# Reading the first expert matrix in memory order for the early lists, and the second in runs of 1 KB to match

## The chip, the core and the metric

The kernel runs on one core of one Trainium2 chip. Its time is the device time of one execution in microseconds (us), as the median of several runs. A profile of one further execution shows the engines: TensorE (PE; PEld are its weight loads), VectorE (DVE), ScalarE (ACT), GpSimd (POOL), and SyncE (SP), which issues most of the DMAs. Each engine works through its own instructions in a fixed order, and waits where a semaphore of another engine or of a DMA has not come yet.

## The reference

Eight sequences of 2496 rows with 256 features go through a spectral layer, and the 19968 rows that come out go through a mixture of eight experts, in which each expert takes at most 2496 rows:

```python
X = np.fft.rfft(x, axis=1)
Yr = X.real @ w_r - X.imag @ w_i + b_r          # and Yi alike
Y = shrink(Yr) + 1j * shrink(Yi)                # by lam = 0.01
x = np.fft.irfft(Y, n=2496, axis=1).reshape(19968, 256)
logits = x @ w_gate                             # 8 columns
# pairs (token, expert) in order of falling logit: a token goes to the
# first expert that still has room (cap = 2496)
for e in range(8):
    h = np.maximum(x[assigned == e] @ w1[e], 0)  # w1[e] is 256 x 1024
    out[assigned == e] = h @ w2[e]               # w2[e] is 1024 x 256
```

The 1024 hidden features of an expert can stand in any order, if the columns of w1 and the rows of w2 have the same one.

## The kernel before

Three kinds of work follow each other and overlap. The spectral layer (`phase_a`) takes the eight sequences as batches, each through small Fourier matrices on PE, with intermediate results that ACT and DVE copy and subtract, POOL in part, and that are written to and read from memory. While the last batches are in it, `Router.early` finds for each expert 512 tokens of the first four batches that surely belong to it: these are the eight early lists, numbered 0 to 7 here. `Router.closing` then settles the experts one after the other, with long searches on DVE that use a tiny count on PE in each step; the tokens of an expert that were not in its early list form its late list, up to 1984 of them.

`Experts.run` works through a list in tiles of 128 tokens and chunks of 512. POOL gathers the rows of the spectral result (L581), PE transposes them (L596), and then comes for each of the eight blocks of 128 hidden features the first product (L611, 512 columns wide, fp32 made of a high and a low part, so six matmuls), an ACT copy with the positive part (L614) and a DVE step for the low part (L615). The second product takes the eight blocks as stationary operands (L627, 24 matmuls of 256 columns for a tile), ACT copies the result out (L630) and POOL scatters it (L634).

`Experts.load` brings in the two matrices of an expert. Each comes in two halves of 512 KB (m = 0, 1) through a ring of two raw tiles of 128 x 1024 (their slots are called xt in the profile, as the spectral part used them before). For an early list SP issues the loads (L557); for a late list the expert is known only on the chip, so POOL gathers rows of 4 KB (L559). Each half is then split: ACT copies it into the high part (L567), which rounds it, and DVE subtracts that from the raw half to get the low part (L568). The first matrix lives in slots called sh, the second in slots called FG. A raw tile is free for the next load when DVE's split of it is done.

How the halves lie matters for the change. A partition of the first matrix's raw half holds one row of w1, 1024 hidden features in memory order. `part` (L562) reads it as `p (k t) -> p t k` with t = 8: for block t the features t, t + 8, t + 16, and so on, 8 elements apart, and writes them side by side. So block t holds the features 8k + t. The second matrix is loaded to fit: partition p takes the rows 8p to 8p + 7 of w2, four in each half, which are one run of 4 KB in memory, and its split reads and writes in order.

The order of the instructions on every engine is set when the program is built. Each step is added to a planner (`Plan`) with an engine, a cost, a position and the buffers that it reads and writes; the planner simulates the engines and emits the steps in the order that comes out. A split costs the planner 0.95 us on ACT and 0.068 + 1024 / 960 us on DVE, for either matrix. ACT's and DVE's queues hold the splits of one list, the L614 and L615 steps of another and the steps of the router one behind the other; PE's holds the counts of the router (L412, L413) among the matmuls.

Of the kernel before, what the change touches and what calls it, by code (L numbers as in the profile page):

```python
# [266 lines left out]
class Kit:  # L267
# [17 lines left out]
    def v(self, n, pos, emit, reads, writes): return self.plan.add('V', 0.068 + n / 960, pos, emit, reads, writes)  # L285
# [252 lines left out]
class Experts:  # L538
# [8 lines left out]
    def load(self, pos, e=None, wi=None):  # L547

        K, plan, v = self.K, self.K.plan, self.K.v
        W1, W2 = K.sb("W1", [128, 2, 2, 1024], F32R), K.sb("W2", [128, 2, 8, 256], F32R)  # L550
        for k in range(2):
            for m in range(2):
                r = K.sb("raw", [128, 1024])
                p = pos + (2 * k + m)
                if e is not None:
                    src = self.w[k][e].rearrange("(p m) f -> p m f", m=2)[:, m] if not k else self.w[k][e].rearrange("(p g m) d -> p g (m d)", g=2, m=4)[:, m]
                    K.dma(p, lambda r=r, src=src: K.nc.sync.dma_start(r.t, src), 524e3, [], [r])  # L557
                else:
                    K.ind(p, lambda r=r, k=k, m=m: K.P.indirect_dma_start(out=r.t, out_offset=None, in_=self.rows[k],  # L559
                                                                          in_offset=bass.IndirectOffsetOnAxis(ap=wi.t[:, m:m + 1], axis=0)), 524e3, [wi], [r])  # L560

                def part(i, k=k, m=m, r=r):  # L562
                    if k: return W2.t[:, i - 1, 4 * m:4 * m + 4] if i else r.t.rearrange("p (m d) -> p m d", m=4)
                    return W1.t[:, i - 1, m].rearrange("p (t k) -> p t k", t=8) if i else r.t.rearrange("p (k t) -> p t k", t=8)
                W = (W1, W2)[k]
                h = plan.buf(None, None)
                plan.add('A', .95, p + 1, lambda part=part: K.A.copy(part(1), part(0)), [r], [W, h])  # L567
                v(1024, p + 1, lambda part=part: K.V.tensor_tensor(part(2), part(0), part(1), op=OP.subtract), [r, h], [W])  # L568
        return W1, W2
# [796 lines left out]
```

## Time and profile before

| | |
|---|---|
| median of 3 runs | 1635.14 us (1633.94 to 1639.24) |
| the profiled execution | 1637.3 us, of which 1635.5 us lie between its first and its last instruction (the span) |
| mean granted TensorE clock | 0.984 |
| instructions | 31215 |
| on the chain that ended last | PE 31%, issue 12%, DVE 6%, POOL 4%, ACT 2%, DMA 2%, by share of the span |
| DMA | 210.64 MB in 134489 packets, mean 129 GB/s |
| the first and the last early split of the first matrix on ACT | 505.1 us and 779.4 us |

Times in the profile count from the span's start. A row of an engine's timeline gives the start and the length in us, the engine, the line of the kernel, the operation, the tile that it writes and those that it reads, the shapes, how many instructions are merged in the row, and in brackets the idle time before it with what ended it. Names of tiles are slots, which different parts of the program share in turn. A PE that is busy is not always a PE at full rate, since its records overlap.

### The profile page before, as it was taken

The page shows a single profiled execution, that of the slowest core. Times are in us where ns is not written, and L with a number is a line of the kernel's source. Part 1 is how long each engine was busy: PE and PEld are TensorE (multiplying, and loading weights), DVE is VectorE, ACT ScalarE, POOL GpSimd, SP SyncE. Part 2 cuts the span into 40 slices and gives each one's busy share as a digit, 9 for nine tenths or more (in the row PEclk, how much of TensorE's full clock was granted, in tenths as well). Part 3 has the DMA queues.
Part 4 walks back from the last instruction along what each step waited for, and adds up shares of the span by engine and source line. Part 5 has one row for each costly group of instructions (what it writes and reads, how often), then busy time and mean ns, then how long its engine had stood idle before and what let it go on. Part 6 is the DMA issues. An engine that isn't in the chain of part 4 may idle for free.

```text
span 1635.5 us, 31215 instructions
## 1 busy us (share of the span) xinstructions
PE 1543.4 (94%) x10980; PEld 1381.9 (84%) x10980; DVE 1181.4 (72%) x3652; ACT 882.4 (54%) x1875; POOL 607.8 (37%) x726
## 2 busy tenths in 40 slices
PE   6999999999999967989899999999999999999997
PEld 3899999998798845878788888888889899889997
DVE  2777777778988885688988989988777766552331
ACT  1568788787688764454634434444344443563331
POOL 1114343343344556212342623534325253473112
PEclk8999999999999988999999999999999999999999
DMA  8877787887686564323221302211122211231000
GB/s 239 237 248 249 224 248 221 251 248 204 216 235 223 165 186 139 113 90 105 90 79 44 101 25 72 71 67 61 44 75 70 72 61 62 84 115 46 20 25 27
DMA packets 134489, 210.64 MB, mean 129 GB/s; under 512 B 31183, under 2 KB 94367, under 8 KB 134129
## 3 DMA queue, kind: packets, MB, share of 16 engines
q1 hardware_dynamic: 112468, 145.53, 29.7%
q0 software_dynamic: 21856, 63.04, 12.3%
q8 instruction: 88, 1.44, 0.4%
q14 instruction: 77, 0.63, 0.1%
HBM read 123.75 MB, written 84.75 MB: 127 GB/s over the span
## 4 chain that ended last, share of the span: by engine, by line
PE 31%; issue 12%; DVE 6%; POOL 4%; ACT 2%; DMA 2%; POOLq 0%; ACTq 0%
PE ps L627 14%; PE ps L611 10%; PE p L611 5%; POOL out_dram L634 3%; DMA xt<-in_moe_w_dram,wi 2%; DVE sh L568 2%; ACT sh L567 1%; PE ps L596 1%; DVE junk L402 1%; DVE FG L568 1%; ACT FG L567 0%; PE p L499 0%; POOL xt L559 0%; DVE yTl L615 0%; ACT ajunk L504 0%
## 5 line engine op out<-in xcount | busy, mean ns | idle before, releaser
L1010 PE MATMUL ps<-wt,xTh 128*128 128x256 f32 x1280 | 242.9, 289 | 0.0
L1010 PEld LDWEIGHTS ps<-wt,xTh 128*128 128x128 f32 x1280 | 200.8, 192 | 2.9 <-issue 0.2
L1010 PE MATMUL ps<-wt,xTl 128*128 128x256 f32 x640 | 181.3, 283 | 0.0
L868 POOL TENSOR_TENSOR s2l<-s2c,s2h 120x512 fp32r<-120x512 f32 (+1 forms) x96 | 118.0, 1233 | 142.7 <-ACT s2h L865 136.5
L634 POOL DMA_INDIRECT out_dram<-xTh,li x64 | 71.2, 1113 | 263.1 <-ACT xTh L630 235.5
L1087 POOL TENSOR_TENSOR yTl<-yr,yTh 128x468 bf16<-128x468 f32 (+1 forms) x88 | 98.8, 1122 | 165.8 <-ACT yTh L1084 114.9
L402 DVE SCALAR_TENSOR_TENSOR junk<-h_m,st,h_AG 128x156 bf16<-128x156 f32 (+1 forms) x472 | 157.9, 380 | 2.5
L1010 PEld LDWEIGHTS ps<-wt,xTl 128*128 128x128 f32 x640 | 122.2, 191 | 0.0
L630 ACT COPY xTh<-ps 128x256 f32<-128x256 f32 x80 | 29.9, 373 | 149.1 <-PE ps L627 127.3
L627 PE MATMUL ps<-FG,yTh 128*128 128x256 f32 (+1 forms) x504 | 108.8, 283 | 0.0
L991 PE MATMUL ps<-FG,sh 128*128 128x128 f32 x640 | 97.0, 282 | 8.4 <-DMA sh<-T 8.0
L991 PEld LDWEIGHTS ps<-FG,sh 128*128 128x128 f32 x640 | 88.4, 195 | 16.5 <-issue 9.5
L630 ACT COPY xTl<-ps 128x256 f32<-128x256 f32 x80 | 29.8, 372 | 126.7 <-PE ps L627 120.6
L634 POOL DMA_INDIRECT out_dram<-xTl,li x64 | 64.9, 1014 | 86.8 <-ACT xTl L630 77.8
L627 PE MATMUL ps<-FG,yTl 128*128 128x256 f32 (+1 forms) x368 | 88.3, 283 | 0.0
L568 DVE TENSOR_TENSOR sh<-xt,sh 128x1024 fp32r<-128x1024 f32 x32 | 69.4, 2182 | 17.9 <-ACT sh L567 17.8
L627 PEld LDWEIGHTS ps<-FG,yTh 128*128 128x128 f32 (+1 forms) x504 | 80.7, 187 | 0.7
L627 PE MATMUL ps<-FG,s2c 128*128 128x256 f32 (+1 forms) x356 | 80.4, 284 | 0.0
L1016 DVE TENSOR_TENSOR ps<-ps,bt 128x512 f32<-128x512 f32 x80 | 55.5, 694 | 30.7 <-PE ps L1010 25.6
L868 DVE TENSOR_TENSOR xl<-xt,xh 117x512 fp32r<-117x512 f32 (+1 forms) x77 | 61.0, 794 | 22.3 <-ACT xh L865 20.2
L1057 PE MATMUL p<-s2h,d 120*117 120x512 f32 (+1 forms) x192 | 76.7, 408 | 0.3 <-DVE s2h L865 0.3
L611 PE MATMUL ps<-y,sh 128*128 128x512 f32 (+1 forms) x187 | 71.5, 400 | 3.6 <-DVE yTl L615 1.6
(648 smaller groups left out, 5162.8 us busy)
## 6 DMA issues: line engine op xcount, KB each, us to landing
sh<-T SPq DMA_DIRECT2D x40, 512.0 KB
T<-s4st SPq DMA_DIRECT2D x80, 256.0 KB
s2c<-T SPq DMA_DIRECT2D x80, 240.0 KB
YD<-yst SPq DMA_DIRECT2D x80, 234.0 KB
T<-s1st SPq DMA_DIRECT2D x73, 240.0 KB
xt<-in_moe_w_dram SPq DMA_DIRECT2D x32, 512.0 KB
xt<-in_x_dram SPq DMA_DIRECT2D x105, 156.0 KB
LG<-lgst SPq DMA_DIRECT2D x80, 21.9 KB
```

What stands on the lines that cost most here:

```text
L402: v(cols + 59, p, lambda k=k: V.scalar_tensor_tensor(junk[k % 2].t[:, 0:cols], H.m[:, 0:cols], c.t[:, k // ng:k // ng + 1], ag(k % ng)[:, ...
L568: v(1024, p + 1, lambda part=part: K.V.tensor_tensor(part(2), part(0), part(1), op=OP.subtract), [r, h], [W])
L611: T.matmul(ps.t[:, 0:w], lhsT=W1.t[:, a, m, 128 * ft:128 * ft + 128], rhs=x_.t[:, 0:w], start=q + m == 0, stop=q + m == 3)
L627: T.matmul(ps.t[0:M], lhsT=a.t[:, 128 * q:128 * q + M], rhs=W2.t[:, w_, ft], start=k == 0, stop=k == 23)
L630: plan.add('A', .27, pos + 1, lambda: A.copy(o.t[0:M], ps.t[0:M]), [ps], [o])
L634: ins = P.indirect_dma_start(out=self.out, out_offset=bass.IndirectOffsetOnAxis(ap=oi.t[0:M, oo + t:oo + t + 1], axis=0), in_=o.t[0:M], in ...
L868: lambda: eng.tensor_tensor(lb[1](), src(), hb[1](), op=OP.subtract), [srcb, hb[0]], [lb[0]])
L991: T.matmul(ps.t[:, i, 128 * dt:128 * dt + 128], lhsT=sh.t[:, k, 128 * dt:128 * dt + 128], rhs=Ft.t[:, k], start=True, stop=True)
L1010: T.matmul(ps3.t[:, i], lhsT=a.t[:, i, dt, o:o + 128], rhs=wt[c].t[:, w, dt], start=n == 0, stop=n == 11)
L1016: plan.add('V', dve(512), pos + 1.282, lambda ps3=ps3: V.tensor_tensor(ps3.t, ps3.t, bt[:, None, :].to_broadcast([128, 2, 256]), op=OP.add ...
L1057: T.matmul(ps.t[0:M, gs_], lhsT=d5[0:k_, a, 0:M], rhs=v.t[0:k_, gs_], start=i == 0, stop=i == 2)
L1087: yq.append(plan.add('P', pool(2 * W), pos + 0.376, lambda yh=yh, yl=yl, yr=yr, W=W: P.tensor_tensor(yl.t[:, :, 0:W], yr.t[:, :, 0:W], yh. ...
```

## The change

Only the loads of the early lists change, in two places that belong together. The split of a first matrix's half reads the raw tile in memory order, so that block t holds the features 128 t to 128 t + 127. The second matrix is loaded to match: partition p takes for block t the row 128 t + p of w2, so a half is made of four runs of 1 KB per partition, 512 runs in place of 128 runs of 4 KB. Both kinds of split write to the same places as before, and the matmuls read the same tiles. The late lists, whose loads are gathered, keep the order that they had.

```diff
                 if e is not None:
-                    src = self.w[k][e].rearrange("(p m) f -> p m f", m=2)[:, m] if not k else self.w[k][e].rearrange("(p g m) d -> p g (m d)", g=2, m=4)[:, m]
-                    K.dma(p, lambda r=r, src=src: K.nc.sync.dma_start(r.t, src), 524e3, [], [r])
+                    src = self.w[k][e].rearrange("(p m) f -> p m f", m=2)[:, m] if not k else self.w[k][e].rearrange("(g m p) d -> p g m d", g=2, m=4)[:, m]
+                    K.dma(p, lambda r=r, src=src, k=k: K.nc.sync.dma_start(r.t.rearrange("p (m d) -> p m d", m=4) if k else r.t, src), 524e3, [], [r])
...
                 def part(i, k=k, m=m, r=r):
                     if k: return W2.t[:, i - 1, 4 * m:4 * m + 4] if i else r.t.rearrange("p (m d) -> p m d", m=4)
-                    return W1.t[:, i - 1, m].rearrange("p (t k) -> p t k", t=8) if i else r.t.rearrange("p (k t) -> p t k", t=8)
+                    return W1.t[:, i - 1, m].rearrange("p (t k) -> p t k", t=8) if i else r.t.rearrange("p (k t) -> p t k" if e is None else "p (t k) -> p t k", t=8)
```

The costs that the planner is given do not change, and the instructions of all engines stand in the same order as before. In SP's queue the sixteen loads of second matrices have another shape (128 x 4 x 256 in place of 128 x 1024); nothing else differs.

## The prediction

> **What bounds the kernel now.** I began with the page. TensorE (PE) is the busiest engine of the whole, at 94%, so what matters is where it is not busy.
>
> ```profile
> PE 1543.4 (94%) x10980; PEld 1381.9 (84%) x10980; DVE 1181.4 (72%) x3652; ACT 882.4 (54%) x1875; POOL 607.8 (37%) x726
> ```
>
> Next the windows: start and end, length, busy time with count of PE, PEld, DVE, ACT and POOL, granted clock, DMA share, GB/s. Six of the eight early lists fall into 640 to 800, the change to the late lists into 800 to 840, the late lists into the rest.
>
> ```profile
> 640.00:800.00 160.00, 147.21 (x961) 129.52 (x960) 126.08 (x415) 79.60 (x115) 37.44 (x55) 0.98 0.31 101
> 800.00:840.00 40.00, 34.50 (x226) 30.00 (x226) 37.57 (x163) 23.20 (x56) 26.63 (x31) 1.00 0.40 122
> 840.00:1635.00 795.00, 772.62 (x5214) 698.57 (x5212) 525.61 (x2068) 328.21 (x751) 292.06 (x403) 1.00 0.18 59
> ```
>
> PE idles 12.8 us in the first stretch, 5.5 us in the second, and 22.4 us in the 795 us behind. From 840 on PE sets the pace, so time won ahead of that should reach the end, if DVE and POOL have the late lists' data ready as much earlier.
>
> The rows of the two split lines come third (minimum, median and maximum ns, first and last start). sh are the slots of the first matrix, FG those of the second.
>
> ```profile
> L567 ACT CAST sh<-xt x32: 2075/2246/2431, 505.1 to 1426.7; 128x1024 fp32r<-128x1024 f32 x32
> L567 ACT CAST FG<-xt x32: 1037/1048/1112, 570.1 to 1447.1; 128x1024 fp32r<-128x1024 f32 x32
> ...
> L568 DVE TENSOR_TENSOR sh<-xt,sh x32: 2003/2186/2354, 507.3 to 1429.0; 128x1024 fp32r<-128x1024 f32 x32
> L568 DVE TENSOR_TENSOR FG<-xt,FG x32: 1205/1225/1950, 574.6 to 1448.2; 128x1024 fp32r<-128x1024 f32 x32
> ```
>
> Shape, types and engines agree; only the order in which the raw tile is read differs. Read 8 elements apart, a split takes 2246 ns on ACT and 2186 on DVE; read in order, 1048 and 1225.
>
> Last, PE's timeline, rows with idle time before them (in brackets, with what ended it): lists 0 and 1 in the spectral part, lists 2 to 7 behind, and one of the first late list.
>
> ```profile
> 510.62 0.39 PE L1027 MATMUL ps<-zl,fg 128*128 128x256 f32 x1 [0.85 <-DVE zl L1020]
> 516.95 0.62 PE L1077 MATMUL pt<-h_idn,yst 117*128 117x117 f32 x4 [0.56 <-DVE yr L1082]
> ...
> 594.10 0.55 PE L1098 MATMUL ps<-yTh,wg 128*32 128x234 bf16 x5 [1.44 <-ACT yTh L1084]
> 596.54 0.55 PE L1098 MATMUL ps<-yTl,wg 128*32 128x234 bf16 x5 [1.85 <-POOL yTl L1087]
> ...
> 650.36 0.39 PE L627 MATMUL ps<-FG,zh 128*128 128x256 f32 x1 [1.58 <-DVE zh L615]
> ...
> 677.93 0.39 PE L627 MATMUL ps<-FG,zh 128*128 128x256 f32 x1 [1.63 <-DVE zh L615]
> ...
> 704.64 0.18 PE L412 MATMUL pt<-cnt,h_ones 128*128 128x4 bf16 x1 [2.34 <-DVE cnt L407]
> ...
> 734.68 0.18 PE L412 MATMUL pt<-cnt,h_ones 128*128 128x4 bf16 x1 [2.32 <-DVE cnt L407]
> ...
> 760.88 0.38 PE L627 MATMUL ps<-FG,yst 128*128 128x256 f32 x1 [1.19 <-DVE yst L615]
> ...
> 784.27 0.18 PE L412 MATMUL pt<-cnt,h_ones 128*128 128x4 bf16 x1 [0.50 <-DVE cnt L407]
> 788.66 0.39 PE L627 MATMUL ps<-FG,yst 128*128 128x256 f32 x1 [1.62 <-DVE yst L615]
> ...
> 819.51 0.18 PE L412 MATMUL pt<-cnt,h_ones 128*128 128x4 bf16 x1 [2.15 <-DVE cnt L407]
> ```
>
> Once in each list PE stands still, for a small DVE step that is itself innocent. ACT's and DVE's own timelines show what that step is queued behind, here for list 4 and, in the last row, list 7:
>
> ```profile
> 696.68 4.58 ACT L567 CAST sh<-xt 128x1024 fp32r<-128x1024 f32 x2 [0.93 <-PE p L611]
> ...
> 699.07 4.34 DVE L568 TENSOR_TENSOR sh<-xt,sh 128x1024 fp32r<-128x1024 f32 x2 [1.25 <-ACT sh L567]
> ...
> 781.66 2.28 DVE L568 TENSOR_TENSOR sh<-xt,sh 128x1024 fp32r<-128x1024 f32 x1 [0.28 <-ACT sh L567]
> ```
>
> DVE waits 1.25 us for ACT's first split and then splits until 703.41; the count that PE wants at 702.30 (704.64 less 2.34) comes behind it.
>
> **The change part by part.** *Splits of the first matrix.* Eight lists with two halves each: I price each at the second matrix's row, since the new reading is in order like its reading. That is 1.20 us less on ACT and 0.96 on DVE per split, 19.2 and 15.4 us in all. This is busy time; what counts is the path. For list 4 DVE's pair now ends at 703.41. With the change ACT's first half ends 1.20 us sooner, and DVE's two save 1.92 more, so the pair ends 3.1 us sooner, at 700.3, ahead of the 702.30 at which PE needs the count. The whole gap goes. The same 3.1 us covers 1.58, 1.63, 2.32 and 1.19. For list 7 DVE itself waits only 0.28 us, so its pair gains 0.28 + 1.92 = 2.2 us against gaps of 0.50 + 1.62 = 2.12: just enough. Sum over lists 2 to 7: 1.58 + 1.63 + 2.34 + 2.32 + 1.19 + 2.12 = 11.2 us. If lists 6 and 7 keep theirs, because DVE is nearly full of routing there, 7.9 are left: the lower bound.
>
> *List 1* sits in the end of the spectral part, where ACT, DVE and POOL hand work on:
>
> ```profile
> 591.49 2.08 ACT L567 CAST sh<-xt 128x1024 fp32r<-128x1024 f32 x1
> ...
> 591.48 4.12 DVE L568 TENSOR_TENSOR sh<-xt,sh 128x1024 fp32r<-128x1024 f32 x2
> ...
> 602.14 3.68 DVE L568 TENSOR_TENSOR FG<-xt,FG 128x1024 fp32r<-128x1024 f32 x2 [0.35 <-ACT FG L567]
> ```
>
> The gaps that end at 594.10 (1.44) and 596.54 (1.85) trace to ACT's copy behind the 591.49 split and to POOL's step behind that copy: 3.3 us at most, nothing at least, if the last batch's own exchange sets the pace. The third row shows that DVE's in-order pair can also take 3.68 instead of 2.45 when it shares the stretch with others. I take 2.3, two thirds. *List 0*: gaps of 0.85 and 0.56 behind its two splits, 1.4 at most, 0 at least if a later wait of the spectral pipeline absorbs it; I take 1.0, nearer the upper end, since PE hardly idles elsewhere around them.
>
> *The clock.* Two windows right behind the gaps at 650.36 and 704.64 show it lowered:
>
> ```profile
> 652.00:656.00 4.00, 4.00 (x23) 3.81 (x23) 0.89 (x2) 0.00 (x0) 1.59 (x4) 0.66 0.66 159
> ...
> 706.00:710.00 4.00, 4.00 (x21) 3.67 (x21) 1.51 (x10) 0.48 (x2) 2.25 (x4) 0.59 0.20 68
> ```
>
> At 0.66 and 0.59 they lose 0.34 x 4 + 0.41 x 4 = 3.0 us of PE time. Without the gaps I expect them to go; since the other four lists' gaps were followed by no such drop, the gap alone does not decide it, and I take 2.4 between 0 and 3.0. [...]
>
> *The loads of the second matrix.* Same 512 KB, in 512 runs of 1 KB instead of 128 of 4 KB. Their rows: the two queues; the landing of gathered loads of the same size; SP's issue of a DMA with 512 runs (64x8), then of list 1's and of one of list 3's loads; and ACT's splits that use them.
>
> ```profile
> q1 hardware_dynamic: 112468, 145.53, 29.7%
> q0 software_dynamic: 21856, 63.04, 12.3%
> ...
> DMA to landing us min/median/max: 3.9/4.8/5.8
> ...
> 536.27 0.58 SPq L351 DMA_DIRECT2D h_ML<-LG  x1
> ...
> 593.55 2.43 SPq L557 DMA_DIRECT2D xt<-in_moe_w_dram  x2
> ...
> 677.31 0.33 SPq L557 DMA_DIRECT2D xt<-in_moe_w_dram  x1
> ...
> 601.05 1.06 ACT L567 CAST FG<-xt 128x1024 fp32r<-128x1024 f32 x1
> ...
> 686.18 2.00 ACT L567 CAST FG<-xt 128x1024 fp32r<-128x1024 f32 x2 [3.14 <-PE ps L627]
> ```
>
> A packet of q1, mean 1294 bytes, takes 0.297 x 16 x 1635.5 / 112468 = 69 ns; one of q0, mean 2884, 147 ns. A load's packets then take 512 x 69 / 16 = 2.2 us instead of 128 x 147 / 16 = 1.2: up to 1 us more; at 147 ns, 4.7, 3.5 more. I take the former, the nearer in size. SP's issue goes from 0.33 to at most 0.58 us, nothing else in its queue presses. Cover: list 3's load is issued at 677.31 and used at 686.18, 8.9 us later, against 4.8 us to land; and DVE's earlier pair issues it 3 us earlier. List 1 is the tightest, 593.55 to 601.05 = 7.5 us, 2.7 over the landing. So 0 on the path; with the cover gone, up to 0.8 us in list 1 (3.5 less 2.7). A gain is excluded, since no step waits for these loads now. PE's and POOL's instructions, and each engine's order, stay as they are.
>
> *Sum*: 11.2 + 2.3 + 1.0 + 2.4 + 0 = 16.9 us. The profiled execution took 1637.3 us (span 1635.5 and 1.8 around it), so 1620.4; it lies 2.2 above the median of the runs, 1635.14. I forecast 1618 for the median. This case's own range: 7.9 gives 1627, and 11.2 + 3.3 + 1.4 + 3.0 = 18.9 gives 1616. A measurement can tell 0.3%, 4.9 us.
>
> **The rivals.** *More than that.* DVE gains 3.1 us per list and PE only 1.2 to 2.3, so DVE enters 800 to 840 ahead and some of PE's 5.5 us there go; 2.15 of them, at 819.51, stand behind the first late list's own split, which stays. That leaves 3.3: 1618 less 3.3 = 1615, with the bounds above down to 1613. For it: DVE is busy 37.57 of 40 there. Against: part of it is a chain of short steps.
>
> *The first late list is not ready.* PE comes to 831 earlier and waits for the routing of late list 0 on the full DVE (37.57 of 40). Then only lists 0 and 1 count, 3.3 us: 1632. Against: that routing runs on the same DVE queue, behind the same splits, and moves up too.
>
> *The split does not get faster*, because something other than the order of reading slows it (the slots, the neighbours): 1635. Against: 32 rows with one median on each side.
>
> *Slower: the 1 KB loads land late.* ACT would stand before the second matrix's split, and DVE and PE behind it, in each of lists 1 to 7. It decides from the point at which a pair lands later than ACT reaches it: 8.9 us after issue plus the 3 it is issued earlier, 12 us. To turn the result it must eat 16.9 + 4.9 = 22 us, 3.1 per list, a landing 15 us after issue against 4.8 now; even 147 ns per packet adds only 3.5 to a load, 7.0 to a pair. Price: 1640 and above.
>
> **How the numbers follow.** Forecast 0.74, more 0.13, not ready 0.06, split unchanged 0.03, slower 0.04. Faster by over 0.3%: 0.74 + 0.13 = 0.87. Within it: 0.06 + 0.03 = 0.09. Slower: 0.04. The range takes the forecast's bounds with the rival that gives more, 1613 to 1627, and 2 us at each end for the spread of the runs (1633.94 to 1639.24): 1611 to 1629.
>
> **What would show it.** In the changed profile L567 and L568 on sh should fall into two groups, 16 near 1.05 and 1.22 us and 16 as now. PE's waits at lists 2 to 7's splits should be gone, with the one at the first late list left; the granted clock in 640 to 720 should be 1.0; PE should reach its late lists some 16 us earlier and idle no more behind that. It is wrong if ACT waits for xt before FG, if PE waits for the first late list's gathers, or if new gaps stand where the old ones were.

## The result and the profile after

The changed kernel takes 1619.62 us (median of 4 runs, 1618.04 to 1622.51) against 1635.14 before. The ratio is 0.990, 95% interval 0.9883 to 0.9917. The profiled execution took 1622.51 us with a span of 1620.7 (before: 1637.3 and 1635.5). One execution among all the runs below, of dve_in_order, fell into a slow state at a granted clock of 0.56 (2486.71 us) and is left out of its numbers.

The first row of the changed kernel's page, then two stretches in windows, each pair of rows the same work before and after. The first stretch runs from the end of the spectral part to the row at which PE has the early lists' splits behind it (L482), the second from there to the first late list's first product; the rows that bound them are shown below.

```profile
PE 1542.3 (95%) x10980; PEld 1381.7 (85%) x10980; DVE 1166.7 (72%) x3652; ACT 864.0 (53%) x1875; POOL 606.4 (37%) x726
```

```profile
634.13:794.10 159.97, 147.36 (x952) 129.30 (x953) 123.91 (x408) 77.71 (x107) 41.48 (x60) 0.98 0.32 104
631.68:776.11 144.43, 142.46 (x952) 126.26 (x952) 112.25 (x408) 63.01 (x107) 41.86 (x60) 1.00 0.36 115
...
794.10:831.31 37.21, 31.54 (x215) 27.27 (x214) 34.80 (x140) 23.81 (x63) 23.53 (x27) 1.00 0.38 117
776.11:816.33 40.22, 34.54 (x214) 29.75 (x213) 34.75 (x140) 23.72 (x63) 24.31 (x28) 0.92 0.36 112
```

ACT's and DVE's busy time over the whole run fell by 18.4 and 14.7 us, PE's by 1.1. In the first stretch PE idles 2.0 us where it idled 12.6, and its busy time falls by 4.9 at a clock of 1.00 instead of 0.98. In the second it idles 5.7 us in both kernels, but is busy 3.0 us longer, at a clock of 0.92 where it was 1.00.

The early splits in the changed kernel, start times 500 to 790 us:

```profile
L567 ACT CAST sh<-xt x16: 1042/1048/1067, 506.9 to 764.8; 128x1024 fp32r<-128x1024 f32 x16
...
L568 DVE TENSOR_TENSOR sh<-xt,sh x16: 1201/1221/1226, 508.2 to 767.1; 128x1024 fp32r<-128x1024 f32 x16
```

The first matrix now costs what the second cost in the rows of before (1048 and 1225). PE's timeline of the changed kernel, rows with idle time before them: one ahead of all splits, three at list 1, one at the end of the spectral part, then the main ones up to the late lists.

```profile
496.49 0.39 PE L1027 MATMUL ps<-zl,FG 128*128 128x256 f32 x1 [0.52 <-DVE zl L1020]
...
593.26 0.55 PE L1098 MATMUL ps<-yTl,wg 128*32 128x234 bf16 x5 [1.73 <-POOL yTl L1087]
596.01 1.13 PE L596 MATMUL ps<-h_idn,y 128*128 128x128 f32 x4 [1.22 <-DVE zl L600]
...
606.91 0.50 PE L611 MATMUL ps<-zh,sh 128*128 128x512 f32 x1 [1.00 <-ACT lgst L1105]
...
631.68 0.51 PE L596 MATMUL ps<-h_idn,xl 128*128 128x128 f32 x2 [1.12 <-DVE yTh L600]
...
659.60 0.50 PE L611 MATMUL ps<-s4st,sh 128*128 128x512 f32 x1 [1.17 <-DVE yTl L615]
...
776.11 0.23 PE L482 MATMUL p<-RD,h_dif 128*128 128x157 f16 x1 [0.66 <-DVE RD L480]
783.03 0.36 PE L499 MATMUL p<-RDd,fg 128*128 128x157 f16 x3 [1.20 <-ACT jl L505]
784.15 0.17 PE L412 MATMUL pt<-cnt,h_ones 128*128 128x4 bf16 x1 [0.75 <-DVE cnt L407]
...
803.01 0.18 PE L412 MATMUL pt<-cnt,h_ones 128*128 128x4 bf16 x1 [2.16 <-DVE cnt L407]
...
816.33 0.50 PE L611 MATMUL ps<-s4st,sh 128*128 128x512 f32 x1 [1.04 <-DVE yTl L615]
```

The gaps at the splits of lists 2 to 7 are gone; the one behind the first late list's split, at 803.01, stays. One gap is new, 1.17 us at 659.60 (0.15 before, at 664.89): PE, now earlier, waits there for a DVE step behind the split of list 2's second matrix, which itself stands behind a routing step that waited for a DMA until 651.64. To say how much came where, the same instructions are looked up in the trace of before:

```profile
494.70 0.39 PE L1027 MATMUL ps<-zl,FG 128*128 128x256 f32 x1 [0.54 <-DVE zl L1020]
...
608.11 0.50 PE L611 MATMUL ps<-zh,sh 128*128 128x512 f32 x1 [1.00 <-ACT lgst L1105]
...
634.13 0.50 PE L596 MATMUL ps<-h_idn,xl 128*128 128x128 f32 x2 [1.28 <-DVE yTh L600]
...
794.10 0.23 PE L482 MATMUL p<-RD,h_dif 128*128 128x157 f16 x1 [0.66 <-DVE RD L480]
...
831.31 0.50 PE L611 MATMUL ps<-s4st,sh 128*128 128x512 f32 x1 [1.03 <-DVE yTl L615]
```

Up to 634.13 the changed kernel has won 2.45 us. From there to the row at 794.10 it takes 144.43 us instead of 159.97: 15.5 won. From there to the row at 831.31 it takes 40.22 instead of 37.21: 3.0 lost. Behind that, 804.37 instead of 804.19. Together 14.8, the difference of the spans. The 3.0 are the clock: idle time is the same, and two drops to half for 3.41 us each, at 786.10 and 803.16, cost up to 3.4 us of full rate. Their rows stand with the prediction's clock term below.

### The profile page after: what moved, and what is told of

It reads as the page before. It is cut to its first block, busy times and chain, and to the rows that moved or that the text cites. A ratio compares the mean times of both kernels' runs of the same rounds, so it can differ in the third digit from the quotient of the medians.

```text
span 1620.7 us, 31215 instructions
## 1 busy us (share of the span) xinstructions
PE 1542.3 (95%) x10980; PEld 1381.7 (85%) x10980; DVE 1166.7 (72%) x3652; ACT 864.0 (53%) x1875; POOL 606.4 (37%) x726
## 3 DMA queue, kind: packets, MB, share of 16 engines
q8 instruction: 88, 1.44, 0.4%
## 4 chain that ended last, share of the span: by engine, by line
PE 61%; issue 13%; DVE 11%; DMA 6%; POOL 4%; ACT 3%; SPq 1%; POOLq 0%; DVEq 0%; ACTq 0%
PE ps L627 16%; PE ps L611 11%; PE ps L1010 11%; PE p L611 5%; PE ps L991 3%; PE ps L1027 3%; POOL out_dram L634 3%; PE p L960 3%; PE p L1057 3%; DMA xt<-in_moe_w_dram,wi 2%; DVE junk L402 2%; PE ps L596 2%; PE pt L1077 1%; DVE FG L568 1%; DMA sh<-in_x_dram 1%
## 5 line engine op out<-in xcount | busy, mean ns | idle before, releaser
L627 PE MATMUL ps<-FG,y 128*128 128x256 f32 (+1 forms) x328 | 74.2, 285 | 0.0
```

Of the source, the lines that this page charges most:

```text
L627: T.matmul(ps.t[0:M], lhsT=a.t[:, 128 * q:128 * q + M], rhs=W2.t[:, w_, ft], start=k == 0, stop=k == 23)
```

## The experiments

The theory: the order of reading makes the split slow, both engines' share of it stands in PE's way, and the 1 KB loads cost nothing. The rivals: the loads matter, for better or worse; or one engine alone accounts for it; or not the order but something near it. Besides the times, the stretch from the row at 634.13 of before (PE, L596) to that at 794.10 (PE, L482) is compared, as it holds lists 2 to 7: 159.97 us before, 144.43 after. Diffs are against the changed kernel. In the first four runs the kernel before took 1713.88 us on the chip used, so there the ratios are compared.

**The split alone, the loads alone.** The first (split_only) puts the 4 KB loads back, the second (loads_only) the old order of the split:

```diff
-                    src = self.w[k][e].rearrange("(p m) f -> p m f", m=2)[:, m] if not k else self.w[k][e].rearrange("(g m p) d -> p g m d", g=2, m=4)[:, m]
-                    K.dma(p, lambda r=r, src=src, k=k: K.nc.sync.dma_start(r.t.rearrange("p (m d) -> p m d", m=4) if k else r.t, src), 524e3, [], [r])
+                    src = self.w[k][e].rearrange("(p m) f -> p m f", m=2)[:, m] if not k else self.w[k][e].rearrange("(p g m) d -> p g (m d)", g=2, m=4)[:, m]
+                    K.dma(p, lambda r=r, src=src, k=k: K.nc.sync.dma_start(r.t, src), 524e3, [], [r])
```

```diff
-                    return W1.t[:, i - 1, m].rearrange("p (t k) -> p t k", t=8) if i else r.t.rearrange("p (k t) -> p t k" if e is None else "p (t k) -> p t k", t=8)
+                    return W1.t[:, i - 1, m].rearrange("p (t k) -> p t k", t=8) if i else r.t.rearrange("p (k t) -> p t k", t=8)
```

> Only the split of the first matrix reads in memory order; the second matrix of the early lists is loaded in 4 KB runs as before (so the hidden features of the two matrices no longer fit each other, and the early lists' rows are other numbers). Theory, the shorter split does it all: as the changed kernel, 1618 to 1622 us. Rival, the 1 KB loads cost something that the split hides: 2 to 4 us faster than the changed kernel. Rival, the loads bring part of the gain: 1624 or more.

> Only the second matrix of the early lists is loaded in runs of 1 KB; the split of the first reads 8 elements apart as before (the hidden features do not fit, the early lists' rows are other numbers). Theory, the loads are hidden: no change against before, within 3 us of it, and the same gaps of TensorE at the lists. Rival, the loads cost: 3 us or more above before, with ACT waiting for xt.

split_only: 1692.96 us, ratio 0.9883 (0.9843 to 0.9923), and its stretch of lists 2 to 7 takes 143.8 us. loads_only: 1715.22, ratio 0.9998 (0.9973 to 1.0023), stretch 160.2. So the split's order makes the difference, and the loads none that these runs can tell.

**Which lists.** The whole change for lists 0 and 1 (lists_0_1), and for lists 2 to 7 (lists_2_7, with `e > 1`); the loads take the same condition.

```diff
-                    return W1.t[:, i - 1, m].rearrange("p (t k) -> p t k", t=8) if i else r.t.rearrange("p (k t) -> p t k" if e is None else "p (t k) -> p t k", t=8)
+                    return W1.t[:, i - 1, m].rearrange("p (t k) -> p t k", t=8) if i else r.t.rearrange("p (t k) -> p t k" if e is not None and e < 2 else "p (k t) -> p t k", t=8)
```

> The whole change for early lists 0 and 1 alone. By the forecast's terms: 1.0 + 2.3 = 3.3 us below before, 1632. By the changed kernel's profile, where the part up to 632 us moved up by 2.5 us, or 4.2 counted from a start that was 1.8 us late: 1631 to 1633. Rival, what is won in the spectral part is lost again before 632: 1635.

> The whole change for early lists 2 to 7 alone. By the forecast's terms: 11.2 for the gaps and 2.4 for the clock, 13.6 us below before, 1621.5. If new drops of the clock at the first late list take the clock's term back, as the changed kernel's profile looks: 11 to 12 below, 1623.5. Rival, gain proportional to the splits: 12 of 16, three quarters of 15.5, 11.6 below, which is no different; then lists 0 and 1 alone tell.

lists_0_1: 1709.38 us, ratio 0.9971 (0.9949 to 0.9993), that is 5.0 us with an interval of 1 to 9; its stretch takes 160.1. lists_2_7: 1695.63, ratio 0.9902 (0.9871 to 0.9934), stretch 145.1. Lists 2 to 7 carry most of the gain; how much the first two carry, 1 us or 5, these runs don't settle.

**Which engine.** Only ACT's copy, or only DVE's subtraction, reads in memory order; the other reads as before. The diff is that of act_in_order; in dve_in_order ACT's copy has `part(0, True)` instead.

```diff
-                def part(i, k=k, m=m, r=r):
+                def part(i, old=False, k=k, m=m, r=r):
...
-                    return W1.t[:, i - 1, m].rearrange("p (t k) -> p t k", t=8) if i else r.t.rearrange("p (k t) -> p t k" if e is None else "p (t k) -> p t k", t=8)
+                    return W1.t[:, i - 1, m].rearrange("p (t k) -> p t k", t=8) if i else r.t.rearrange("p (k t) -> p t k" if e is None or old else "p (t k) -> p t k", t=8)
...
-                v(1024, p + 1, lambda part=part: K.V.tensor_tensor(part(2), part(0), part(1), op=OP.subtract), [r, h], [W])
+                v(1024, p + 1, lambda part=part: K.V.tensor_tensor(part(2), part(0, True), part(1), op=OP.subtract), [r, h], [W])
```

> The changed kernel, but only ACT's copy of the first matrix reads in order; DVE's subtraction reads 8 elements apart (high and low parts no longer belong together, the early lists' rows are other numbers). Theory, what counts is when DVE's pair ends: DVE starts 1.2 us sooner and its two then take 2.19 each, so the pair ends 1.2 sooner; of the gaps at lists 2 to 7 go 1.2 each for lists 2 to 5, 1.19 and 0.28: 6.3 us, and with lists 0 and 1 some 8 below before, 1627. Rival, ACT's busy time is what matters (19.2 of 34.6 us saved): 8.6 below. Rival, ACT is hidden: 1635 still.

> The changed kernel, but only DVE's subtraction reads the raw first matrix in order; ACT's copy reads 8 elements apart (the early lists' rows are other numbers). Theory, the end of DVE's pair counts: its second half cannot start before ACT's second ends, 4.5 us after ACT starts, so the pair ends at 4.5 + 0.1 + 1.2 = 5.8 us instead of 6.7: 0.9 us per list, some 5.5 us at lists 2 to 7 and 1 to 2 more at 0 and 1: 1628 to 1629. Rival, DVE's busy time is what matters: its two save 1.9 per list, gaps go almost whole: 1623 or less.

act_in_order: 1626.71 us, ratio 0.9932 (0.9909 to 0.9955), stretch 150.6, 9.4 less than before. dve_in_order: 1629.49, ratio 0.9941 (0.9925 to 0.9957), stretch 151.9, 8.1 less. The stretch in windows, of act_in_order and then of dve_in_order, and list 4's gap with ACT alone in order:

```profile
631.96:782.51 150.55, 144.01 (x951) 126.49 (x952) 123.63 (x408) 63.25 (x108) 42.34 (x60) 1.00 0.36 111
```

```profile
634.51:786.38 151.87, 144.27 (x952) 126.53 (x952) 112.66 (x408) 77.46 (x107) 41.04 (x60) 1.00 0.36 110
```

```profile
697.40 0.18 PE L412 MATMUL pt<-cnt,h_ones 128*128 128x4 bf16 x1 [1.15 <-DVE cnt L407]
```

At list 4 the gap falls from 2.34 to 1.15, by the 1.2 us that ACT's first half ends sooner. PE's idle time in the stretch falls from 12.6 us to 6.5 and 7.6, by 6.1 and 5.0; the expectations, worked out from the end of DVE's pair, were 6.3 and 5.5. So the gaps come from the chain through both engines, ACT's first half and then DVE's two: each engine shortens it, neither removes it. In idle time the two gains add up to 11.1, near the 10.6 of the whole change. The lengths of the stretch add up to 17.5 against 15.5, since the 3.1 to 3.3 us of busy time that go at a clock of 1.00 are in both.

**How far apart.** The split reads elements 4, and 2, apart instead of 8; the loads are in runs of 4 and 2 KB to match. The diff is that of step_2; step_4 has g=2, t=4 in the split, and loads `(g p m) d -> p g (m d)`.

```diff
-                    src = self.w[k][e].rearrange("(p m) f -> p m f", m=2)[:, m] if not k else self.w[k][e].rearrange("(g m p) d -> p g m d", g=2, m=4)[:, m]
+                    src = self.w[k][e].rearrange("(p m) f -> p m f", m=2)[:, m] if not k else self.w[k][e].rearrange("(h g p m) d -> p h g (m d)", h=2, g=2, m=2)[:, m]
...
-                    return W1.t[:, i - 1, m].rearrange("p (t k) -> p t k", t=8) if i else r.t.rearrange("p (k t) -> p t k" if e is None else "p (t k) -> p t k", t=8)
+                    return W1.t[:, i - 1, m].rearrange("p (t k) -> p t k", t=8) if i and e is None else W1.t[:, i - 1, m].rearrange("p (g t k) -> p g t k", g=4, t=2) if i else (r.t.rearrange("p (k t) -> p t k", t=8) if e is None else r.t.rearrange("p (g k t) -> p g t k", g=4, t=2))
```

> Early lists with another order that fits: within each half of the hidden features block m holds the features 4k + m, so the split of the first matrix reads 4 elements (16 bytes) apart, and the second matrix is loaded in runs of 4 KB as before. Same result as the reference. If the split's price grows with every step above 1: between 1.05 and 2.25 us on ACT, and a time between 1619.6 and 1635. If a step of 16 bytes is as good as none: as the changed kernel. If it is as bad as 32 bytes: as before.

> The split of an early first matrix reads elements 2 apart (8 bytes), and the second matrix is loaded in runs of 2 KB to match; the result is the reference's. Step 8 (32 bytes) costs 2246 ns on ACT and 2186 on DVE, step 4 (16 bytes) 2127 and 2056, step 1 1048 and 1225. If the cost is set by how many 16-byte pieces a split touches (two elements of a piece in a row here, one at steps 4 and 8), step 2 lies near the cost of step 1, 1.05 to 1.2 us on ACT and 1.2 to 1.35 on DVE, all gaps of lists 2 to 7 go, and the time is 1619 to 1622, that of the change. If any reading out of order costs a second pass, it stays at 2.0 to 2.1 us, gaps of 1.2 to 1.8 us stay as at step 4, and the time is 1629 to 1632.

step_4: 1631.28 us, ratio 0.996 (0.9943 to 0.9976), stretch 153.8. step_2: 1620.35, ratio 0.9906 (0.9882 to 0.993), stretch 144.7 (629.64 to 774.36). Their early splits, first 4 and then 2 apart:

```profile
L567 ACT CAST sh<-xt x16: 2037/2068/2090, 504.5 to 772.0; 128x1024 fp32r<-128x1024 f32 x16
...
L568 DVE TENSOR_TENSOR sh<-xt,sh x16: 1987/2026/2059, 506.6 to 774.3; 128x1024 fp32r<-128x1024 f32 x16
```

```profile
L567 ACT CAST sh<-xt x16: 1116/1132/1186, 507.3 to 763.1; 128x1024 fp32r<-128x1024 f32 x16
...
L568 DVE TENSOR_TENSOR sh<-xt,sh x16: 1199/1222/2097, 508.7 to 765.3; 128x1024 fp32r<-128x1024 f32 x16
```

So it is not order as such. Read 2 elements apart, 8 bytes, a split took 1132 ns on ACT and 1222 on DVE, nearly the 1048 and 1221 of reading on; 4 apart, 16 bytes, 2068 and 2026; 8 apart, 32 bytes, 2234 and 2164 (medians of the sixteen early splits of step_2, the change, step_4 and before). The cost jumps between a step of 8 bytes and one of 16, by 83% on ACT and 66% on DVE, and rises by 8% and 7% from there to 32. This is where the first case of step_2's expectation put the jump; why it lies there, these four steps don't show.

**Shorter runs.** The second matrix in runs of 256 (runs_256, the diff) and of 64 bytes (runs_64, with c=16), 2048 and 8192 to a load.

```diff
-                    src = self.w[k][e].rearrange("(p m) f -> p m f", m=2)[:, m] if not k else self.w[k][e].rearrange("(g m p) d -> p g m d", g=2, m=4)[:, m]
-                    K.dma(p, lambda r=r, src=src, k=k: K.nc.sync.dma_start(r.t.rearrange("p (m d) -> p m d", m=4) if k else r.t, src), 524e3, [], [r])
+                    src = self.w[k][e].rearrange("(p m) f -> p m f", m=2)[:, m] if not k else self.w[k][e].rearrange("(g m p) (c d) -> p g c m d", g=2, m=4, c=4)[:, m]
+                    K.dma(p, lambda r=r, src=src, k=k: K.nc.sync.dma_start(r.t.rearrange("p (c m d) -> p c m d", c=4, m=4) if k else r.t, src), 524e3, [], [r])
```

> The changed kernel with the second matrix of the early lists loaded in runs of 256 bytes, 2048 to a load (the columns stand in another order in the tile, so the early lists' rows are other numbers). Theory, loads have about 9 to 12 us from issue to use and cost nothing while they land inside it: 2048 packets at 69 ns at the most are 8.8 us per load on 16 engines, 17.7 for a pair, so ACT would wait for xt some 5 us per list, and the time goes to 1635 or above; at half that price per packet it just fits and stays at 1620 to 1624. Either way ACT's wait for xt tells where the cover ends.

> As the change, but each early second matrix is loaded in runs of 64 bytes, 8192 to a load; the early lists' rows come out as other numbers. By the queue's rows, the 24576 more packets of the 256-byte version took (0.312 x 1618.3 - 0.301 x 1620.7) x 16 / 24576 = 11 ns each. At that price a load takes 5.3 us longer than at 1 KB and mostly hides under the cover of 8.9 to 12 us: 1620 to 1630, with waits of ACT before the second matrix's split. At 69 ns a packet, the price of the prediction, it takes 33 us longer, and the six lists behind the spectral part wait some 20 us each: 1700 and above. If SP's issue grows with the number of runs, SP's queue shows it first.

runs_256: 1622.85 us, ratio 0.9909 (0.9873 to 0.9944), stretch 145.2 against the change's 144.4, and ACT never waits for an early load. runs_64: 1650.69, ratio 1.0103 (1.0063 to 1.0142), slower than the kernel before. The queue of the loads (packets, MB, share of 16 engines' span), of the changed kernel, runs_256 and runs_64:

```profile
q1 hardware_dynamic: 118612, 145.53, 30.1%
```

```profile
q1 hardware_dynamic: 143188, 145.53, 31.2%
```

```profile
q1 hardware_dynamic: 241492, 145.53, 35.6%
```

Each further packet took (0.312 x 1618.3 - 0.301 x 1620.7) x 16 / 24576 = 11 ns, and at 64 bytes (0.356 x 1648.2 - 0.312 x 1618.3) x 16 / 98304 = 13 ns. That is far under the 69 ns of a packet's mean before; cutting the same bytes finer added 1.1 and then 4.4 points to the queue's share. What 64 bytes do is seen on ACT, which waits for loads (us, times, longest), on PE, and on SP:

```profile
ACT FG L567 <- DMA xt<-in_moe_w_dram: 18.2, 8, 3.8
```

```profile
613.28 1.04 PE L1077 MATMUL ps<-h_idn,yst 117*128 117x117 f32 x4 [6.93 <-ACT yst L1059]
...
674.35 0.80 PE L611 MATMUL p<-s4st,sh 128*128 128x512 f32 x1 [6.71 <-DVE yTh L615]
```

```profile
653.81 6.47 SPq L557 DMA_DIRECT2D xt<-in_moe_w_dram  x2
660.45 6.73 SPq L351 DMA_DIRECT2D h_ML<-LG  x1
```

The gap at 613.28 is the prediction's slower rival: ACT's two splits just ahead of it, of list 1's second matrix, wait 3.76 and 3.10 us for their loads. But it takes runs sixteen times shorter than the change's. The gap at 674.35 comes another way, through SP's queue: the issue of two of the loads and of the DMA behind them takes 6.47 and 6.73 us there, 1.84 and 0.59 in the changed kernel. So the router's logits, next in that queue, come late, a DVE step waits 14.76 us for them, and the step that PE needs stands behind it. The time lies over the 1630 that 11 ns a packet gave at most, and under the 1700 of 69 ns: 13 ns a packet is not all. SP's longest issue of one load rose from 0.94 to 5.03 us; how much of the whole loss is SP's, these runs don't show.

**The late lists too.** late_order reads the late lists' first matrices in memory order as well; late_1k also gathers their second matrices to match, in four gathers of 1 KB rows in place of one of 4 KB. The first diff is in late_order; late_1k has the same order where the flag `fine` is set, as the late lists' call does. The second is in late_1k, whose closing step also works out the eight row numbers (8 wa - 7 p + 128 t for block t).

```diff
-                    return W1.t[:, i - 1, m].rearrange("p (t k) -> p t k", t=8) if i else r.t.rearrange("p (k t) -> p t k" if e is None else "p (t k) -> p t k", t=8)
+                    return W1.t[:, i - 1, m].rearrange("p (t k) -> p t k", t=8) if i else r.t.rearrange("p (t k) -> p t k", t=8)
```

```diff
-                    K.ind(p, lambda r=r, k=k, m=m: K.P.indirect_dma_start(out=r.t, out_offset=None, in_=self.rows[k],
-                                                                          in_offset=bass.IndirectOffsetOnAxis(ap=wi.t[:, m:m + 1], axis=0)), 524e3, [wi], [r])
+                    for q in range(4 if k and fine else 1):
+                        K.ind(p, lambda r=r, k=k, m=m, q=q: K.P.indirect_dma_start(out=r.t[:, 256 * q:256 * q + 256] if k and fine else r.t, out_offset=None, in_=self.rows[2] if k and fine else self.rows[k],
+                                                                                   in_offset=bass.IndirectOffsetOnAxis(ap=wi.j.t[:, 4 * m + q:1 + 4 * m + q] if k and fine else wi.t[:, m:m + 1], axis=0)), 131e3 if k and fine else 524e3, [wi.j if k and fine else wi], [r])
```

> As the change, and the late lists' first matrices are split in memory order too; their second matrices are still gathered in the old order, so the late lists' rows come out as other numbers. No instruction is added or moved. It bounds what the remaining 16 slow splits cost. If the pause of 2.16 us and the two clock drops at the first late list come from its split, both go and the time is 1614 to 1617, 3 to 5 us under the change; if behind 825 us PE itself sets the pace, nothing more than 1 us comes from lists 1 to 7 of the late ones. If the drops come from PE's load alone, the gain is 2 us or less, 1617 to 1620.

> As late_order, with the late lists' second matrices gathered in runs of 1 KB to match, so that the result is the reference's: eight gathers instead of two for each late list, 48 more on POOL (938 to 984 ns each, some 46 us of POOL time over 800 us in which it is busy 37% of the time), and three tiny DVE steps for each list's row numbers. The planner orders the late part anew. If the gathers hide as the early loads do, the time is within 1 us of late_order; if POOL's gathers of tokens stand behind the 6 more, PE waits up to 6 us in the first late list and up to some us in the others: 1618 to 1630.

late_order: 1602.29 us, ratio 0.9794 (0.9772 to 0.9816). late_1k, in which the two matrices fit each other again: 1609.18, ratio 0.9832 (0.9812 to 0.9852), faster than the change; beside step_2 on the same chip it is 11 us less. My expectation for late_order was far too small: I looked for 3 to 5 us under the change, and it is 17. The same work in windows, of the changed kernel and of late_order, from the first late list's first product to a row of the late lists further on:

```profile
816.33:1437.26 620.93, 608.17 (x4111) 545.88 (x4112) 482.92 (x2013) 277.12 (x646) 242.21 (x326) 1.00 0.20 66
```

```profile
806.57:1415.05 608.48, 605.71 (x4111) 546.09 (x4112) 470.56 (x2013) 261.56 (x646) 238.51 (x329) 1.00 0.21 67
```

PE idled 12.8 us there and idles 2.8. The rows of the changed kernel in 840 to 1400 with over 1.2 us before them, and a later one as a mark; then the only two of late_order there with more than 0.5, between the same two marks:

```profile
1090.62 0.50 PE L611 MATMUL ps<-y,sh 128*128 128x512 f32 x1 [1.53 <-DVE s2c L615]
1188.17 0.50 PE L611 MATMUL ps<-y,sh 128*128 128x512 f32 x1 [1.60 <-DVE yTl L615]
...
1287.66 0.50 PE L611 MATMUL p<-s1st,sh 128*128 128x512 f32 x1 [1.40 <-DVE s2c L615]
1291.43 0.47 PE L611 MATMUL ps<-yst,sh 128*128 128x448 f32 x1 [1.26 <-DVE s1st L615]
...
1437.26 0.39 PE L596 MATMUL ps<-h_idn,yst 128*128 128x128 f32 x1 [1.16 <-DMA yst<-YD,li]
```

```profile
806.57 0.50 PE L611 MATMUL ps<-s4st,sh 128*128 128x512 f32 x1 [1.04 <-DVE yTl L615]
...
890.99 0.47 PE L611 MATMUL p<-yTl,sh 128*128 128x448 f32 x1 [0.54 <-DVE yTl L615]
...
1272.03 0.48 PE L611 MATMUL ps<-yst,sh 128*128 128x448 f32 x1 [0.97 <-DVE s1st L615]
...
1415.05 0.39 PE L596 MATMUL ps<-h_idn,yst 128*128 128x128 f32 x1 [1.13 <-DMA yst<-YD,li]
```

From the row at 816.33 (shown above) to that at 1437.26 the changed kernel takes 620.9 us, late_order from 806.57 to 1415.05 608.5: 12.4 us come behind the first late list's split. In the stretch of that split, 40.22 us in the changed kernel, late_order takes 36.31, 3.9 less: the gap of 2.16 is gone, and one of the two clock drops does not come. Together these are 16.3 of the 17 us. The two spans differ by 22.1; the other 5.8 lie ahead, where both kernels have the same code, and are the spread of single executions. So a PE busy 98% of a stretch, with its 2% of idle time spread thin, still met the same slow split in list after list. late_1k gives back 7 of the 17 us, between the two cases that were expected for it; it has 48 more gathers on POOL, three more DVE steps per list and a newly planned order of all engines, and which of these it is stays open.

## Why the prediction was right

**The split's price** was right: 1048 and 1221 ns measured, 1048 and 1225 taken from the second matrix's row. A row of the same shape and types that is read in order was a fair price, and step_2 (1132 and 1222 ns) and step_4 (2068 and 2026) show on what it rests.

**Lists 2 to 7**, 11.2 us forecast: PE's idle time in the stretch fell from 12.6 to 2.0 us, by 10.6. All six lists' gaps went, as worked out, and the lower bound of 7.9 wasn't needed; the new gap of 1.17 us, further on in list 2, took a tenth of the term back. The stretch became 15.5 us shorter: the other 4.9 are busy time, 3.4 of them the clock (next point), and 1.5 that these runs don't explain.

**The clock**, 2.4 us forecast, was the one term that failed in sum: the two drops of before did go, but two came at the first late list and took 3.0 back. What comes ahead of a drop can be read from windows of 3.41 us, the length of each of these four, laid so that a drop fills one. Before, the window ahead of the drop at list 4 and the drop; the two that share list 5's gap; the two that share the gap at 819.51:

```profile
702.49:705.90 3.41, 1.26 (x12) 1.26 (x13) 3.04 (x13) 0.60 (x2) 0.00 (x0) 1.00 0.82 296
705.90:709.31 3.41, 3.41 (x15) 3.12 (x15) 1.61 (x10) 0.58 (x2) 2.25 (x4) 0.50 0.13 46
...
729.79:733.20 3.41, 2.56 (x12) 1.76 (x10) 3.41 (x7) 2.27 (x4) 0.00 (x0) 1.00 0.45 144
733.20:736.62 3.42, 1.94 (x16) 1.90 (x17) 3.35 (x19) 0.52 (x2) 0.20 (x1) 1.00 0.53 168
...
815.12:818.54 3.42, 2.24 (x18) 1.95 (x16) 3.21 (x8) 0.87 (x4) 2.88 (x3) 1.00 0.40 126
818.54:821.95 3.41, 2.44 (x21) 2.44 (x22) 3.15 (x25) 0.37 (x1) 2.72 (x4) 1.00 0.57 186
```

In the changed kernel, the windows ahead of the two drops and the drops:

```profile
782.68:786.10 3.42, 1.77 (x10) 1.37 (x10) 3.39 (x21) 3.34 (x14) 2.89 (x4) 1.00 0.39 121
786.10:789.51 3.41, 3.41 (x11) 2.39 (x11) 3.41 (x17) 1.98 (x8) 2.50 (x4) 0.50 0.77 221
...
799.75:803.16 3.41, 1.25 (x13) 1.05 (x12) 3.41 (x18) 0.01 (x1) 2.89 (x4) 1.00 0.58 191
803.16:806.58 3.42, 3.42 (x19) 3.42 (x18) 3.02 (x19) 0.37 (x1) 2.15 (x4) 0.50 0.60 200
```

The drops of one trace lie whole steps of 3.41 us apart: 16 before, from 651.28 to 705.90, and 5 after, from 786.10 to 803.16. List 4's gap of 2.34 us lies in one window, in which PE is busy for 1.26 us, and a drop follows; list 5's of 2.32 is shared by two, and none does. The gap of 2.15 at the first late list is shared by two windows before and lies in one in the changed kernel. In all fourteen traces together, before and after among them, the stretch from 640 to 850 us has 830 such windows at full clock: a drop followed each of the 21 in which PE was busy, by the profile's busy time, for less than 47%, none of those with more than 55%, and 3 of the 15 between. So in these traces it is not the length of a gap but how much of PE's idle time falls into one window of the trace's grid of 3.41 us. Where the grid lies against the work is luck, as far as they show: the gaps at the first late list, 1.20, 0.75, 0.55 and 2.1 to 2.2 us, stand alike in the traces of before, act_in_order, dve_in_order, step_2, runs_256, step_4 and the change, and bring no drop in the first two, one in the next three, two in the last two. The two new drops are thus not shown to be the change's, and a clock term that is read from one trace is the luck of that trace.

Without the clock's 2.4 the forecast would have been 1620.6, which is 1.0 us over the measured 1619.62; my 1618 is 1.6 under: the time alone doesn't tell whether the term belongs.

**Lists 0 and 1**, 1.0 and 2.3 forecast: 2.45 us measured at 634.13, or 4.2 if the 1.8 us by which the changed kernel's execution lay behind ahead of the first split (494.70 against 496.49) are only the spread of the runs. In list 1 the gap that ACT's copy ended (1.44) went, while the one that POOL ended stayed (1.85, now 1.73) and a new one of 1.22 came at 596.01; by 606.91 PE was 1.2 us ahead of before (608.11). That looks as if more of list 1's gaps belonged to the spectral part's own exchange than I took, but one execution can't say so: from the first of these rows to the end of the spectral part the changed kernel takes 135.19 us, late_order with the same code 132.25.

**The loads**, 0 forecast: right by loads_only, 0.9998. Their price was mis-sized without harm: I took 69 ns a packet and bounded it by 147, where a further packet cost 11 to 13 in runs_256 and runs_64.

**The rivals.** More than that: no; from the row at 776.11 to that at 816.33 PE idles 5.7 us as before, and the 2.16 gap behind the late list's split stayed as said. Not ready: no, PE waits for none of the first late list's gathers. Behind the late lists' begin nothing changed, as said, but the prediction's reading that PE sets the pace there was only half the truth: late_order won 12.4 us there.

The sum, in spans: 2.45 + 15.5 - 3.0 - 0.2 = 14.8 measured, 16.9 forecast. The mechanism, PE's gaps behind the chain of both splits, came out to within 0.6 us of 11.2; that the total came so near owes something to luck, since lists 0 and 1 are within the spread and the clock's drops fell as the grid lay.

## What to carry to other kernels

Before costing an elementwise step by its shape, look at how far apart it reads: rows of one shape with two medians, one about twice the other (2246 and 1048 ns on ACT here), point to it, and if the order of a dimension is free, the layout can be changed where the data is loaded. A gap of PE ended a chain through several engines here; shortening one link took away what the end of the chain moved (at list 4, ACT's 1.2 us of a gap of 2.34). Add up such gains in idle time, and keep the clock's share apart, since a drop that goes with any of them is counted in each (stretches of 9.4 and 8.1 against 15.5, idle times of 6.1 and 5.0 against 10.6). PE, busy 98% of the late lists' stretch, still waited there for the same slow step in list after list (12.4 us, by late_order); the rest of a change made for one set of lists should be looked for in the others.

## What the hardware showed that I had not expected

- Reading fp32 from a tile of 128 x 1024, ACT took 1048 ns at a step of 1, 1132 at 2, 2068 at 4 and 2234 at 8; DVE's subtraction 1221, 1222, 2026 and 2164. The jump lies between steps of 8 and 16 bytes (runs: the change, step_2, step_4, before).
- Cutting a load of 512 KB into 2048 runs of 256 bytes instead of 512 of 1 KB added 11 ns for each further packet to the queue's time and nothing measurable to the kernel; 8192 runs of 64 bytes made it slower than before the change (ratio 1.0103, 1.0063 to 1.0142), and one SP issue of such a load took up to 5.03 us.
- From 640 to 850 us the granted clock fell to half for one or more windows of 3.41 us, whole steps of 3.41 us apart in one trace, behind windows in which PE was busy for less than about half (all 21 under 47%, none over 55%, 3 of the 15 between). A gap of 2.34 us in one window brought a drop, one of 2.32 us shared by two brought none.
